# New duration estimates in the list schedule of an attention and two-MLP kernel

## The chip, the cores and the metric

The kernel runs on one core of a Trainium2 chip. Its engines are TensorE (PE, with its weight loads shown apart as PEld), VectorE (DVE), ScalarE (ACT), GpSimd (POOL) and SyncE (SP), which issues the transfers. Each engine executes its own instructions in a fixed order and waits for the others through semaphores. The metric is the time of one execution on the device, in microseconds; several executions are timed and their median is taken.

## The reference

The inputs q, k and v have 2 batches, 8 heads, 768 positions and 64 elements per head. `proj` (64 x 6) hashes every row of q and k into one of 64 buckets, and attention is allowed only inside a bucket. Two linear blocks follow on 1536 tokens of 512 elements.

```python
q_bits = (np.einsum('bhsd,dk->bhsk', q, proj) > 0)      # k_bits alike
mask = q_bucket[:, :, :, None] == k_bucket[:, :, None, :]
scores = np.where(mask, scale * np.matmul(q, k.transpose(0, 1, 3, 2)), -1e9)
attn = softmax(scores)                                  # row maximum taken off first
x = np.matmul(attn, v)                                  # to (1536, 512)
x = ((x @ w1) * (x @ w2)) @ w3 @ w_out                  # d_ff 1024
x = (sigmoid(x @ w_gate) * (x @ w_val)) @ w_out2        # d_ff 1536
```

The weights of the two blocks arrive as 64-bit floats.

## The kernel before, in words

**Attention.** There are 16 heads and six query tiles of 128 per head, so 96 score tiles. Each head's q and k are split into a high and a low part that TensorE can multiply in one pass (`prep`, L389 to L417), the hash bits are computed with three small matmuls per half (`gps`, L387) and are appended to the operands by copies from SBUF to SBUF (L405 to L415). For each score tile TensorE makes four matmuls into one of only two PSUM tiles `s` (L462, L465); VectorE takes the row maximum and prepares the scalars `sm` (L472, L473); ScalarE makes the exponential `e` (L483); TensorE transposes it in pieces of 128 x 128 (`tp`, L516); ScalarE and VectorE copy it out as high and low part `pt` (L519, L521); TensorE multiplies with v (`av`, L534). The two first heads skip the low part.

**Filler.** Between the attention's steps lies work on the weights. Every piece of 128 x 512 weights is loaded by SP into a staging tile `st` (L320) and decoded from 64 bits: ScalarE takes the absolute value and the low bits (L336, L337), GpSimd keeps the sign (L338) and limits the value (`min`, L339), VectorE shifts it (L340) and combines the two (L345, which the profile names a custom instruction). `gen_fill` decodes `w3` and `w_out` and multiplies them into one matrix, `wacc` (L589): ScalarE copies the high part of `w_out` to `wo` (a helper, L278) and GpSimd computes its low part (L584). `gen_first` then decodes `w1` and `w2` and begins with the first 512 tokens of the first linear block (`p` and `y`, L694). 40 of the 76 decodes belong to these two.

**The rest.** `moe` works through the other tokens and the second block, nearly all matmuls of 512 columns (`pa`, `pb` and `m`, L694). It is emitted after the list schedule has been made and isn't part of it.

**What sets the order.** `order_engines` (L47 to L228) takes all instructions emitted so far, that is attention, filler and the beginning of the first block, and simulates their execution. Whenever an engine is free in that simulation, it takes the ready instruction with the lowest priority number: attention's steps and the filler carry numbers that grow from step to step. An instruction is ready when those it depends on have ended, plus a delay by pair of engines (`step`, L93), and when its tile's buffer is free. How long each instruction takes comes from `cost(k)` (L76), and for a transfer from L218 to L221: it begins after a delay or when the transfer before it is done, moves so many bytes per ns, and is known 900 ns later. The order in which each engine took its instructions is then tied down with dependencies (L226 to L228). The durations therefore decide nothing but the order: on the chip each engine keeps it and waits where the next instruction isn't ready. `rings` names for every tile its pool; `psT` and `psS` are the two pools in PSUM, all others lie in SBUF.

Of the kernel before, what the change touches and what calls it, by code (L numbers as in the profile page):

```python
# [29 lines left out]
class Tiles:  # L30
# [3 lines left out]
    rings = {}  # L34
# [12 lines left out]
def order_engines(tc):  # L47
# [8 lines left out]
    rings = Tiles.rings  # L56
    N = len(ins)

    def count(x):
        n = 1  # L60
        for _, c in list(x.ap)[1:]:
            n *= c
        return n

    def region(x):

        b = getattr(x, "bass_ap", None)
        if b is None or b.tensor.name not in rings:
            return None
        ap = [list(p) for p in b.ap]  # L70
        es = mybir.dt.size(b.dtype)
        p0, f0 = divmod(b.offset, ap[0][0]) if ap[0][0] else (0, b.offset)
        f1 = f0 + sum((c - 1) * abs(st) for st, c in ap[1:]) + 1
        return b.tensor.name, p0, p0 + ap[0][1], f0 * es, f1 * es

    def cost(k):  # L76
        i, e, op = ins[k], eng[k], type(ins[k]).__name__
        rd = [x for x in i.ins if hasattr(x, "ap")]
        n = max([count(i.outs[0])] + [count(x) for x in rd[:1]])
        if e == "PE":  # L80
            passes = 1 if "float32r" in str(rd[0].dtype) else 2 if n == 128 else 4
            return n / 2.4 * passes + 2.5
        if e == "Activation":
            return 971 if n == 768 else 50 + n * 0.836
        if e == "Pool":
            return 60 + n * 2.3
        if e == "DVE":
            if op in ("InstTensorTensor", "InstTensorReduce") or (op == "InstTensorScalarPtr" and len(rd) > 1 and count(rd[1]) > 8):
                return 69 + n * 1.04
            return 585 if op == "InstTensorScalarPtr" and n == 384 else 69 + n * 0.52  # L90
        return 600

    step = {("Activation", "DVE"): 145, ("Activation", "PE"): 200, ("Activation", "Pool"): 170, ("DVE", "Activation"): 132,  # L93
# [53 lines left out]
    def blocked(k):  # L147
        for t in opens.get(k, ()):
            g = rings[t][0]
            if slots[g] <= 0 or queue[g][taken[g]] != t:  # L150
                return g
            if g[0] == "mw" and pools.get("wtmp"):
                return "wtmp"
        return None
# [4 lines left out]
    dma = 0.0  # L159

    def wake(g):
        for k in waiting.pop(g, ()):
            heapq.heappush(ready[eng[k]], (ins[k].bass_priority, k))

    def post(t, what, x):
        heapq.heappush(events, (t, next(tick), what, x))
# [4 lines left out]
    while events:  # L171
        now = events[0][0]
        while events and events[0][0] <= now:
            _, _, what, x = heapq.heappop(events)
            if what == "ready":
                heapq.heappush(ready[eng[x]], (ins[x].bass_priority, x))
            elif what == "slot":
                g = rings[x][0]
                slots[g] += 1
                pools[g[0]] -= 1  # L180
                wake(g)
                if not pools[g[0]]:
                    wake(g[0])
            elif what == "end":
                for u in ends[x]:
                    left[u] -= 1
                    at[u] = max(at[u], now + step.get((eng[x], eng[u]), 60))
                    if not left[u]:
                        post(at[u], "ready", u)
                for t in held.get(x, ()):  # L190
                    todo[t] -= 1
                    if not todo[t]:
                        post(now + 200, "slot", t)
        again = True
        while again:
            again = False
            for e in ranks:
                while free[e] <= now and ready[e]:
                    _, k = heapq.heappop(ready[e])
                    g = blocked(k)  # L200
                    if g is not None:
                        waiting.setdefault(g, []).append(k)
                        continue
                    for t in opens.get(k, ()):
                        g = rings[t][0]
                        slots[g] -= 1
                        taken[g] += 1
                        if slots[g] > 0 and waiting.get(g):
                            wake(g)
                            again = True  # L210
                    order[e].append(k)
                    for u in begins[k]:
                        left[u] -= 1
                        at[u] = max(at[u], now)
                        if not left[u]:
                            post(at[u], "ready", u)
                    free[e] = done = now + cost(k)
                    if e == "SP":  # L218
                        n = count(ins[k].outs[0]) * list(ins[k].outs[0].ap)[0][1] * mybir.dt.size(ins[k].outs[0].dtype)
                        dma = max(now + 1080, dma) + n / 360  # L220
                        done = dma + 900  # L221
                    post(done, "end", k)
                    post(free[e], "free", k)
# [8 lines left out]
def lsh_attention_moe_moe2_kernel(  # L232
# [654 lines left out]
    for _ in first:  # L887
        pass
    order_engines(tc)
    prio(0, 200000)  # L890
    att_ctx.close()
# [44 lines left out]
```

## Time and profile before

| what | us or share |
|---|---|
| median of 3 runs (lowest to highest) | 823.49 (823.34 to 823.85) |
| the profiled execution's own time | 825.39 |
| span of its instructions | 823.6 |
| TensorE busy (its weight loads) | 789.6 (660.2) |
| VectorE busy | 467.7 |
| ScalarE busy | 505.9 |
| GpSimd busy | 428.2 |
| mean granted TensorE clock | 0.985 |

The busy times are shares of the whole span. A row of a stage table gives the same numbers for one stretch, so that idle time is the stretch's length less the busy time. Attention and filler lie before about 366 us, the rest after it. In a timeline each line gives start, duration, engine, source line, the tile written and the tile read; the bracket at its end tells how long the engine sat idle just before and which instruction ended the idle time.

### The profile page before, as it was taken

To read this page: it belongs to the slowest core of one execution; us is meant where nothing else is said; L and a number is where in the kernel's file an instruction comes from. 1 tells how busy PE (TensorE), PEld (TensorE's weight loads), DVE (VectorE), ACT (ScalarE), POOL (GpSimd) and SP (SyncE) were. 2 spreads that over 40 slices of the span, in tenths; PEclk is the share of its full clock that TensorE was granted. 3 is DMA by queue.
4 is the path that set the end of the run, shared out by engine and by line. 5 is a ranking of instruction groups with operands and counts; after the bars stand their busy time and mean duration, and the time that the engine had idled before them with its cause. 6 is when DMAs were issued, how large, how long until landed. Compare 5 with 4: busy or idle time off the path is not lost.

```text
span 823.6 us, 11474 instructions
## 1 busy us (share of the span) xinstructions
PE 789.6 (96%) x3984; PEld 660.2 (80%) x3984; DVE 467.7 (57%) x794; ACT 505.9 (61%) x912; POOL 428.2 (52%) x454
## 2 busy tenths in 40 slices
PE   4799899999899999999999999999999999999998
PEld 3577788888799889878888888888888888888886
DVE  6537788887889988985454444654522222222222
ACT  5578888787788887885465656775534333343332
POOL 4567666665556555478355546677532323232320
PEclk9899899999999999999999999999999999999999
DMA  7745557544455644131022213334001000010001
GB/s 247 204 116 164 169 154 197 139 132 114 122 151 155 162 103 129 62 112 52 1 76 77 77 52 101 109 138 138 2 1 51 1 1 0 1 52 0 1 1 51
DMA packets 28585, 74.45 MB, mean 90 GB/s; under 512 B 6128, under 2 KB 8432, under 8 KB 28528
## 3 DMA queue, kind: packets, MB, share of 16 engines
q1 hardware_dynamic: 28528, 73.73, 30.1%
q8 instruction: 31, 0.51, 0.3%
q14 instruction: 26, 0.21, 0.1%
HBM read 52.83 MB, written 3.19 MB: 68 GB/s over the span
## 4 chain that ended last, share of the span: by engine, by line
PE 86%; ACT 5%; DVE 5%; issue 2%; POOL 1%; DMA 1%; SPq 1%; ACTq 0%; POOLq 0%; DVEq 0%
PE m L694 18%; PE pa L694 17%; PE pb L694 17%; PE av L534 8%; PE tp L516 6%; PE p L694 4%; PE wacc L589 4%; PE s L462 4%; PE s L465 3%; PE y L694 3%; ACT e L483 2%; DVE s L472 2%; PE gps L387 2%; DVE pt L521 1%; DMA st<-in_moe_w_dram 1%
## 5 line engine op out<-in xcount | busy, mean ns | idle before, releaser
L734 DVE TENSOR_TENSOR pb<-pb,a 128x512 f32<-128x512 f32 x52 | 36.3, 699 | 179.5 <-PE pb L694 176.2
L472 DVE TENSOR_REDUCE s<-s 128x1 f32<-128x768 f32 x96 | 91.8, 959 | 28.2 <-PE s L465 15.4
L483 ACT ACTIVATE e<-s,sm 128x768 f32<-128x768 f32 x96 | 95.3, 994 | 17.0 <-DVE sm L473 16.3
L516 PE MATMUL tp<-idf,e 128*128 128x128 f32 x576 | 103.2, 279 | 0.0
L688 POOL TENSOR_TENSOR wal<-xall,wah 128x512 fp32r<-128x512 f32 x36 | 46.9, 1304 | 106.2 <-ACT wah L278 106.2
L694 PE MATMUL pa<-x,wah 128*128 128x512 f32 x320 | 99.2, 390 | 0.0
L694 PE MATMUL pb<-x,wbh 128*128 128x512 f32 x320 | 98.6, 389 | 0.0
L338 POOL TENSOR_SCALAR dr<-st 128x512 bf16<-128x512 f32 x76 | 72.3, 961 | 43.4 <-issue 22.6
L519 ACT ACTIVATE pt<-tp 128x512 fp32r<-128x512 f32 (+1 forms) x144 | 82.1, 596 | 20.4 <-PE tp L516 19.1
L534 PE MATMUL av<-pt,spv 128*128 128x256 f32 (+1 forms) x576 | 88.1, 303 | 1.0 <-DVE pt L521 0.9
L521 DVE TENSOR_TENSOR pt<-tp,pt 128x512 fp32r<-128x512 f32 x126 | 83.2, 682 | 9.9 <-ACT pt L519 9.5
L534 PEld LDWEIGHTS av<-pt,spv 128*128 128x128 f32 (+1 forms) x576 | 74.5, 187 | 11.8 <-DVE pt L521 4.0
L516 PEld LDWEIGHTS tp<-idf,e 128*128 128x128 f32 x576 | 73.8, 144 | 9.8 <-issue 1.5
L462 PE MATMUL s<-bk,bq 128*128 128x384 f32 x192 | 64.0, 389 | 14.6 <-ACT e L483 12.8
L589 PE MATMUL wacc<-wo,t 128*128 128x512 f32 x192 | 66.8, 425 | 7.3 <-ACT wo L278 4.7
L694 PEld LDWEIGHTS pa<-x,wah 128*128 128x128 f32 x320 | 60.1, 188 | 13.2
L694 PEld LDWEIGHTS pb<-x,wbh 128*128 128x128 f32 x320 | 60.1, 188 | 12.6
L339 POOL TENSOR_SCALAR da<-da 128x512 f32<-128x512 f32 x76 | 48.1, 637 | 37.8 <-ACT da L336 29.2
L694 PE MATMUL pa<-x,wal 128*128 128x512 f32 x160 | 62.5, 391 | 1.1 <-POOL wal L688 1.1
L694 PE MATMUL pb<-x,wbl 128*128 128x512 f32 x160 | 62.5, 390 | 0.0
L465 PE MATMUL s<-ak,aq 128*128 128x384 f32 x192 | 61.2, 381 | 0.0
L337 ACT ACTIVATE dr<-st 128x512 int16<-128x512 uint32 x76 | 59.7, 786 | 0.1
(137 smaller groups left out, 1794.2 us busy)
## 6 DMA issues: line engine op xcount, KB each, us to landing
st<-in_moe_w_dram SPq DMA_DIRECT2D x32, 512.0 KB, 4.1
st<-in_moe_w_out_dram SPq DMA_DIRECT2D x20, 512.0 KB, 4.2
st<-in_moe_w_gate_dram SPq DMA_DIRECT2D x12, 512.0 KB, 3.3
st<-in_moe_w_val_dram SPq DMA_DIRECT2D x12, 512.0 KB, 3.2
qk<-in_qk_dram SPq DMA_DIRECT2D x15, 384.0 KB, 4.0
rr<-row SPq DMA_DIRECT2D x16, 192.0 KB, 3.5
out_dram<-o SPq DMA_DIRECT2D x12, 256.0 KB, 2.0
ak<-aq SPq DMA_DIRECT2D x15, 192.0 KB, 2.5
```

Source lines behind the costliest of these rows:

```text
L337: act.activation(out=r.bitcast(I16)[:, 0::2], in_=lw, func=AF.Copy, scale=2.0 ** -29)
L338: pool.tensor_scalar(out=r.bitcast(BF16)[:, 1::2], in0=f(hw), scalar1=0.0, scalar2=1.0, op0=ALU.mult, op1=ALU.mult)
L462: pe.matmul(s[:, half, :HS], lhsT=m["bq"][:, qs], rhs=m["bk"][:, ks], start=True, stop=False)
L465: pe.matmul(s[:, half, :HS], lhsT=m["aq"][:, qs], rhs=m["ak"][:, ks], start=False, stop=True)
L472: dve.tensor_reduce(out=one[:, 1:2], in_=s[:, :, :HS], op=ALU.max, axis=AX.XY, negate=True)
L483: act.activation(out=e.rearrange("p (a c) -> p a c", a=2), in_=s[:, :, :HS], func=AF.Exp, bias=sm[:, 1:2], scale=sm[:, 0:1], accum_out=su_ ...
L516: pe.transpose(ps[:, i * P:(i + 1) * P], e_t[g - g % 2 + a][:, c * P:(c + 1) * P], idf)
L519: act.activation(out=dh, in_=src, func=AF.Copy)
L521: dve.tensor_tensor(out=d, in0=src, in1=f(dh), op=ALU.subtract)
L534: pe.matmul(acc[:w.shape[1], :2 * P].rearrange("p (a t) -> p a t", a=2), lhsT=w, rhs=r[:, :, c], start=(c == 0 and i == 0), stop=(c == NT ...
L589: pe.matmul(acc, lhsT=t3[x][:, j], rhs=wo[y][:, j], start=(j == 0 and n == 0), stop=(j == NF1 - 1 and n == 2))
L694: mm = pe.matmul(ps, lhsT=lhs[x], rhs=rhs[y], start=start and n == 0, stop=stop and n == 2)
```

## The change

Two places of `order_engines` get other numbers. `cost` now tells apart whether the operand that is read or the tile that is written lies in PSUM (`banks`), gives GpSimd's subtractions and its other operations formulas of their own, gives VectorE's custom instruction a fixed duration, and shifts TensorE's durations by the kind of matmul. A transfer is taken to begin 1900 ns instead of 1080 after its issue and to move 300 instead of 360 bytes per ns. The instructions, the buffers, the priorities and the delays between engines are as before.

```diff
@@ -77,17 +77,22 @@
         i, e, op = ins[k], eng[k], type(ins[k]).__name__
         rd = [x for x in i.ins if hasattr(x, "ap")]
         n = max([count(i.outs[0])] + [count(x) for x in rd[:1]])
+        banks = [x for x in rd + [i.outs[0]] if (region(x) or ("",))[0] in rings and rings[region(x)[0]][0][0] in ("psT", "psS")]
         if e == "PE":
             passes = 1 if "float32r" in str(rd[0].dtype) else 2 if n == 128 else 4
-            return n / 2.4 * passes + 2.5
+            return n / 2.4 * passes + (16 if passes == 1 else -12 if passes == 2 else 4)
         if e == "Activation":
-            return 971 if n == 768 else 50 + n * 0.836
+            return 971 if n == 768 and banks else 50 + n * (0.836 if banks else 1.0)
         if e == "Pool":
-            return 60 + n * 2.3
+            if op == "InstTensorTensor":
+                return 40 + n * 2.4 if n < 768 else 2200
+            return 100 + n * 1.15
         if e == "DVE":
+            if op == "InstCustomDveAnt":
+                return 720
             if op in ("InstTensorTensor", "InstTensorReduce") or (op == "InstTensorScalarPtr" and len(rd) > 1 and count(rd[1]) > 8):
-                return 69 + n * 1.04
-            return 585 if op == "InstTensorScalarPtr" and n == 384 else 69 + n * 0.52
+                return 69 + n * (1.04 if banks else 1.4)
+            return 585 if op == "InstTensorScalarPtr" and n == 384 else 69 + n * 0.6
         return 600
@@ -217,7 +222,7 @@
                     if e == "SP":
                         n = count(ins[k].outs[0]) * list(ins[k].outs[0].ap)[0][1] * mybir.dt.size(ins[k].outs[0].dtype)
-                        dma = max(now + 1080, dma) + n / 360
+                        dma = max(now + 1900, dma) + n / 300
                         done = dma + 900
```

## Rows read from the trace of the kernel before

**Rows 1.** Stage table: stretch, length, busy us (instructions) per engine, PEclk, DMA share, GB/s.
```profile
0.00:20.00 20.00, 9.19 (x26) 7.62 (x26) 11.87 (x36) 11.40 (x18) 9.20 (x18) 1.00 0.76 248
20.00:48.00 28.00, 22.06 (x103) 16.64 (x104) 14.52 (x26) 18.07 (x35) 16.55 (x21) 0.82 0.69 189
...
76.00:100.00 24.00, 18.73 (x108) 15.99 (x108) 18.76 (x35) 19.37 (x37) 15.79 (x21) 0.86 0.58 170
...
200.00:232.00 32.00, 27.80 (x166) 24.85 (x166) 24.62 (x45) 23.95 (x46) 18.25 (x20) 0.89 0.38 108
232.00:366.00 134.00, 133.60 (x857) 119.67 (x856) 120.18 (x216) 113.06 (x218) 76.75 (x90) 1.00 0.46 127
366.00:823.60 457.60, 452.82 (x1965) 368.28 (x1963) 177.37 (x264) 218.83 (x370) 206.28 (x182) 1.00 0.13 45
```

**Rows 2.** TensorE's waits, whole span: total us, times, longest us.
```profile
PE s L462 <- ACT e L483: 12.8, 9, 3.4
...
PE wacc L589 <- ACT wo L278: 4.7, 2, 2.9
...
PE wacc L589 <- POOL wo L584: 0.9, 1, 0.9
```

**Rows 3.** Timeline of GpSimd, 30 to 47 us: start, duration, instruction.
```profile
31.10 0.61 POOL L339 TENSOR_SCALAR da<-da 128x512 f32<-128x512 f32 x1
...
32.91 0.61 POOL L339 TENSOR_SCALAR da<-da 128x512 f32<-128x512 f32 x1
```

**Rows 4.** Timeline of VectorE in the same stretch.
```profile
32.68 0.67 DVE L409 TENSOR_SCALAR ft<-gps,thr 128x384 fp32r<-128x384 f32 x1
35.38 0.97 DVE L472 TENSOR_REDUCE s<-s 128x1 f32<-128x768 f32 x1 [2.02 <-PE s L465]
...
37.48 0.42 DVE L340 TENSOR_SCALAR da<-da 128x512 uint32<-128x512 uint32 x1
...
38.01 0.69 DVE L345 CUSTOM_DVE_ANT_0 wor<-da,dr 128x1024 uint16<-128x1024 uint16 x1
```

**Rows 5.** Groups of decode steps, 0 to 366 us: busy us, mean ns, idle before.
```profile
L338 POOL TENSOR_SCALAR dr<-st 128x512 bf16<-128x512 f32 x41 | 34.2, 836 | 4.1 <-issue 1.2 <-DVE w3f L345 1.1
...
L339 POOL TENSOR_SCALAR da<-da 128x512 f32<-128x512 f32 x40 | 25.1, 626 | 35.2 <-ACT da L336 28.5 <-DMA qk<-in_qk_dram 4.7
L340 DVE TENSOR_SCALAR da<-da 128x512 uint32<-128x512 uint32 x40 | 22.9, 572 | 7.1 <-POOL da L339 6.9
```

**Rows 6.** Timeline of TensorE, 36 to 47 us.
```profile
39.42 0.79 PE L589 MATMUL wacc<-wo,t 128*128 128x512 f32 x1 [2.91 <-ACT wo L278]
```

**Rows 7.** Timeline of three engines, 84 to 90.6 us.
```profile
84.28 0.61 POOL L339 TENSOR_SCALAR da<-da 128x512 f32<-128x512 f32 x1
...
86.56 0.97 DVE L472 TENSOR_REDUCE s<-s 128x1 f32<-128x768 f32 x1 [1.07 <-PE tp L516]
87.77 0.67 DVE L345 CUSTOM_DVE_ANT_0 wor<-da,dr 128x1024 uint16<-128x1024 uint16 x1
...
89.15 0.54 PE L589 MATMUL wacc<-wo,t 128*128 128x512 f32 x1 [1.81 <-ACT wo L278]
```

**Rows 8.** Transfers by line: issues, KB each, median us from issue to landing.
```profile
st<-in_moe_w_dram SPq DMA_DIRECT2D x32, 512.0 KB, 4.1
...
ak<-aq SPq DMA_DIRECT2D x15, 192.0 KB, 2.5
```

**Rows 9.** Timeline of VectorE and ScalarE, 12 to 16 us.
```profile
13.50 0.22 DVE L473 SCALAR_TENSOR_TENSOR sm<-lim,s 128x2 f32<-128x2 f32 x1
...
14.54 0.97 ACT L483 ACTIVATE e<-s,sm 128x768 f32<-128x768 f32 x1
```

**Rows 10.** Timeline of VectorE and GpSimd, 224 to 227 us.
```profile
224.21 2.24 DVE L632 TENSOR_TENSOR xl<-xall,xh 128x512 fp32r<-128x512 f32 x2
...
225.99 1.10 POOL L338 TENSOR_SCALAR dr<-st 128x512 bf16<-128x512 f32 x1
```

**Rows 11.** Timeline of TensorE, 219 to 226 us.
```profile
221.20 0.44 PE L462 MATMUL s<-bk,bq 128*128 128x384 f32 x1 [2.26 <-ACT e L483]
```

## The prediction

> **What bounds the kernel now.** I read the stage table first. TensorE is the engine that is full: from 20 us on it has work in 78 to nearly 100% of each stretch, and from 232 to 366 us it is idle for only 0.4 us of 134 although VectorE is busy 120.2 us there [rows 1]. From 366 us on, where most of the work lies outside the list schedule, it loses 4.8 us of 457.6 [rows 1]. The set of instructions is the same after the change, so TensorE's work is the same, and the time can move only by TensorE's holes and by the work that runs at the lower clock behind a hole. The holes of the scheduled part are 10.8 us (0 to 20), 5.9 (20 to 48), 5.3 (76 to 100), 4.2 (200 to 232) and 0.4 (232 to 366); the granted clock is 0.82, 0.86 and 0.89 in the middle three, which is at most 0.18 x 28 = 5.0, 0.14 x 24 = 3.4 and 0.11 x 32 = 3.5 us, and 1.00 in the others [rows 1]. That is what a better order can win.
>
> The waits of TensorE say what ends the holes: the score tile waits for the exponential (12.8 us in nine waits), the folded weight product `wacc` waits for ScalarE's copy of a decoded `w_out` (4.7 in two) and for GpSimd's low part (0.9) [rows 2]. The second kind hangs on the decode of weights, and that is the work whose model cost changes most.
>
> **The change, part by part.** It adds no work. It changes the numbers from which each engine's order is drawn up.
>
> GpSimd's two decode steps are the big edit. A step of 512 elements cost 60 + 512 x 2.3 = 1238 ns and now costs 100 + 512 x 1.15 = 689; the pair falls from 2475 to 1378 ns. In the trace GpSimd finished the `min` steps of two decodes at 31.71 and 33.52 us [rows 3]. VectorE was idle for 2.02 us, from 33.35 to 35.38, yet took the shift of the first decode only at 37.48, behind its reductions [rows 4]. The pair is 836 + 626 = 1462 ns in the trace [rows 5]. The old price is 1.0 us above that for the first decode and 2.0 for both, so the old model has them done near 32.7 and 35.5 and had reason to put the reductions first; by the new one they end at 31.6 and 33.4, and shift and combine (0.42 and 0.69 us [rows 4]) fit into the hole. The decoded `w_out` then exists near 34.5 instead of 38.7 (38.01 + 0.69), and ScalarE's copy can follow at once. TensorE's wait of 2.91 us for that copy [rows 6] goes. What is late next there is GpSimd's low part, which TensorE can pass by with transposes. The lower clock costs at most 5.0 us in this stretch [rows 1], and this wait is half of its holes. I take a third, 1.6 us, since the other holes come first and would lower the clock without it. Sum of the first hole: 4.5 us, bounds 0 (it is taken by something else) and 2.9 + 5.0 = 7.9.
>
> The hole at 88 us has the same form: GpSimd was done with a `min` step at 84.89, VectorE stood idle 1.07 us before a reduction at 86.56 and combined the `w_out` only at 87.77; TensorE waited 1.81 us for what follows [rows 7] and 0.9 for GpSimd's part of it [rows 2]. By the old price that step ends 0.6 us later, by the new one within 0.1 us of the measured place. The combine moved into the idle 1.07 us brings the copy forward by up to 1.8 us. I take 2.0 us for wait and clock together, between 0 and 2.7 + 3.4 = 6.1, nearer the low end since the next hole, the scores waiting for the exponential behind it, stays.
>
> Transfers: a 512 KB weight was expected 1080 + 1456 + 900 = 3.44 us after issue and is now 1900 + 1748 + 900 = 4.55, with the transfers one behind another at 300 instead of 360 bytes per ns; the measured median is 4.1. An SBUF copy of 192 KB goes from 2.53 to 3.46, measured 2.5 [rows 8]. So weights are now nearer the truth and the copies farther. At the start ScalarE took two decode steps ahead of the first exponential, whose scalars were ready at 13.72; it began at 14.54 [rows 9]. A model that expects the weights later may turn these round: 0 to 0.8 us, taken 0.4. The copies feed the next head: expected 0.93 us too late, their consumers are put later in TensorE's order. With other work ahead of them that costs nothing; uncovered it is 15 heads x 0.93 = 14 us. I take 0, since in 134 us TensorE idles 0.4 [rows 1]. SP issues in an order drawn from the same model, but no instruction of SP is added, and a load moved on SP is moved with its decode.
>
> ScalarE's copies from SBUF rise by 84 ns (478 to 562), VectorE's combine from 601 to 720 if counted at the 1024 elements that the trace shows (from 335 at 512), its shift from 335 to 376. TensorE: 1464 one-pass matmuls up by 13.5 ns = 19.8 us, 576 transposes down by 14.5 = 8.4, so the modelled TensorE gets 11.4 us longer, which gives the other engines more room in the model. None of these is a cost by itself. They reshuffle everything after the first hole, and the reshuffling has a price: VectorE now meets GpSimd with no reserve. Measured, the two GpSimd steps take 1462 ns against 1378, and VectorE waited for them only 6.9 us in 40 decodes [rows 5]. The reserve that goes is 40 x (1462 - 1378) = 3.4 us of VectorE, and one new hole with its half clock is worth some 2.5 more (the 200 to 232 stretch has 3.5 of clock for two holes). Bounds 0 and 5.9 us, taken 2.9, the middle, as no row shows how much of VectorE's lateness reaches TensorE.
>
> Here a rule bears on the change. While VectorE made two subtractions in 2.24 us, a GpSimd step beside them took 1.10 us [rows 10], where its mean is 0.84 [rows 5]. The Trainium skill's page "SBUF — State Buffer" (Who interferes with whom) says that a VectorE instruction with two SBUF inputs and a GpSimd instruction that reads SBUF shut each other out, whichever comes first running to its end. By that rule no fixed duration fits these two engines, and the trace agrees with it in the rows just named; the time it would give is that of the second rival below.
>
> The holes near 219 us stay: they come when the first phase of the filler ends and four copies of the next phase's input go ahead of an exponential, for which TensorE waits 2.26 us [rows 11]. Their prices rise alike, their priority doesn't change. Term 0, between -2 and +2.
>
> Sum: -4.5 - 2.0 - 0.4 + 2.9 = -4.0 us. The profiled execution took 825.39 us, 1.8 outside its span of 823.6; that gives 821.4 in its terms. The median of the runs is 823.49, 1.9 below the profiled one, so I predict 819.5.
>
> **The rivals.** First, the reshuffling gives back what the two holes give, or the priorities and not the durations set the order there: 823.5. For it: the stretch from 232 us, the longest, has nothing to win. Against: two of the holes have a visible cause in a wrong price.
>
> Second, slower. VectorE's decode steps are placed where GpSimd is expected, GpSimd is late because the two block each other, and VectorE, in order, keeps reduction, scalars and exponential waiting behind the decode, in the stretch from 232 us, where it is busy 120.2 of 134 us. Price: the whole 5.9 us, with the first two holes unchanged: 823.5 + 5.9 = 829.4. It decides from the point where VectorE's waits for GpSimd's `min` step pass about 14 us, twice today's. For it: the longer step beside two subtractions. Against: GpSimd has idle time before most of these steps, and can run ahead.
>
> Third, larger: with transfers and decode right, the holes of 20 to 48 and 76 to 100 us close whole with their clock, about two thirds of 5.9 + 5.0 + 5.3 + 3.4 = 19.6 (hole and half clock overlap), so 13 us: 810.5. Against: scores still wait for exponentials, which have only two score tiles.
>
> **How the numbers follow.** Forecast 0.39 (815 to 822 by itself), no net change 0.17, slower 0.31, larger gain 0.13. A difference within 0.2%, 1.65 us, can't be told from none, so faster means below 821.8 and slower above 825.1. Faster: 0.39 + 0.13 = 0.52, with 0.01 of the no-change case for its edge: 0.53. Same 0.16, slower 0.31. The range goes from 809 (the larger gain) to 829.5 (the slower rival); it leaves out a full 14 us on the copies and a gain beyond 15.
>
> **What would show it.** Right: TensorE's waits for ScalarE's `w_out` copies fall from 4.7 us to under 2; the shift follows GpSimd's `min` within about 1 us near 33 us; the clock in 20 to 48 us above 0.9. Wrong: VectorE's wait for `min` above 14 us, new holes between 232 and 366 us, where 0.4 us stand now, or a clock below 1.00 there. The prediction fails if the holes only change place.

## The result and the profile after

The changed kernel takes 815.98 us (median of four executions, 812.86 to 816.30) against 823.67 for the kernel before, a ratio of 0.990 with a 95% interval of 0.987 to 0.992. The forecast was the right way and 4.0 us; the kernel gained 7.7. The profiled execution happens to be the quickest of the four, 812.86 us with a span of 811.1, and that of before is slower than its median, so the two traces differ by 12.5 us and what is read from them overstates the gain.

The stage table of the kernel after, with the columns of [rows 1], and under it TensorE's largest waits as in [rows 2]:

```profile
0.00:20.00 20.00, 9.98 (x27) 7.31 (x28) 13.26 (x38) 12.26 (x19) 9.87 (x18) 0.87 0.76 266
20.00:48.00 28.00, 26.01 (x138) 20.20 (x137) 17.66 (x29) 23.16 (x45) 23.89 (x30) 0.91 0.82 214
...
76.00:100.00 24.00, 23.43 (x148) 20.05 (x146) 22.81 (x44) 21.25 (x42) 17.74 (x24) 1.00 0.82 230
...
200.00:232.00 32.00, 28.27 (x185) 25.07 (x184) 29.53 (x51) 27.06 (x53) 17.26 (x22) 1.00 0.60 161
232.00:366.00 134.00, 132.09 (x810) 115.04 (x809) 117.40 (x201) 111.66 (x215) 81.33 (x87) 1.00 0.45 120
```

```profile
PE s L467 <- ACT e L488: 9.7, 8, 2.5
...
PE wacc L594 <- ACT wo L283: 2.0, 1, 2.0
```

The hole of 20 to 48 us fell from 5.9 to 2.0 us and that of 76 to 100 from 5.3 to 0.6, where the clock is whole again [rows 1]. In return 232 to 366 us has 1.9 us of hole where it had 0.4. TensorE executes 138 and 148 matmuls in the two early stretches instead of 103 and 108: work came forward. What brought it is seen at 28 us, in a timeline of four engines of the kernel after (compare [rows 3, 4, 6]):

```profile
28.12 0.61 POOL L344 TENSOR_SCALAR da<-da 128x512 f32<-128x512 f32 x1
...
28.77 0.43 DVE L345 TENSOR_SCALAR da<-da 128x512 uint32<-128x512 uint32 x1 [2.66 <-POOL da L344]
...
29.34 0.76 POOL L343 TENSOR_SCALAR dr<-st 128x512 bf16<-128x512 f32 x1
...
29.40 1.18 DVE L350 CUSTOM_DVE_ANT_0 wor<-da,dr 128x1024 uint16<-128x1024 uint16 x1
...
30.18 0.88 POOL L344 TENSOR_SCALAR da<-da 128x512 f32<-128x512 f32 x1
...
30.62 0.63 ACT L283 ACTIVATE wo<-wor 128x512 fp32r<-128x512 f32 x1 [1.02 <-DVE wor L350]
...
31.30 0.50 PE L594 MATMUL wacc<-wo,t 128*128 128x512 f32 x1 [1.99 <-ACT wo L283]
```

VectorE takes the shift 0.04 us after GpSimd's `min` ends (28.73), not 5.8 us after it as before. The first `wacc` runs at 31.3 us instead of 39.4. The eight decodes of `w_out` show how far this goes. The two fences are the combine step of these decodes, before and after, with the shortest, median and longest duration in ns and the first and last start in us:

```profile
L345 DVE CUSTOM_DVE_ANT_0 wor<-da,dr x8: 672/693/1448, 38.0 to 87.8; 128x1024 uint16<-128x1024 uint16 x8
```

```profile
L350 DVE CUSTOM_DVE_ANT_0 wor<-da,dr x8: 686/920/1807, 29.4 to 65.3; 128x1024 uint16<-128x1024 uint16 x8
```

All eight are done 22.5 us earlier. The attention ends earlier too: VectorE's last low part `pt` starts at 344.8 us instead of 356.7:

```profile
L521 DVE TENSOR_TENSOR pt<-tp,pt x126: 640/681/693, 68.3 to 356.7; 128x512 fp32r<-128x512 f32 x126
```

```profile
L526 DVE TENSOR_TENSOR pt<-tp,pt x126: 669/681/695, 63.4 to 344.8; 128x512 fp32r<-128x512 f32 x126
```

That is 11.9 of the 12.5 us between the two profiled executions. Behind it the two differ by 0.6 us.

### The profile page after: what moved, and what is told of

Its sections match the earlier page's. It is cut to its first block, busy times and chain, and to the rows that moved or that the text cites. A ratio compares the mean times of both kernels' runs of the same rounds, so it can differ in the third digit from the quotient of the medians.

```text
span 811.1 us, 11465 instructions
## 1 busy us (share of the span) xinstructions
PE 785.6 (97%) x3984; PEld 653.5 (81%) x3984; DVE 470.0 (58%) x794; ACT 505.5 (62%) x912; POOL 431.4 (53%) x454
## 4 chain that ended last, share of the span: by engine, by line
PE 80%; DVE 8%; ACT 4%; POOL 4%; DMA 2%; issue 2%; SPq 1%; ACTq 0%; DVEq 0%; POOLq 0%
PE m L699 18%; PE pa L699 18%; PE pb L699 18%; PE av L539 6%; PE tp L521 5%; PE p L699 4%; PE wacc L594 3%; PE s L467 3%; PE s L470 2%; DVE s L477 2%; PE y L699 2%; DVE pt L526 2%; ACT e L488 1%; PE gps L392 1%; DMA st<-in_moe_w_dram 1%
## 5 line engine op out<-in xcount | busy, mean ns | idle before, releaser
L521 PE MATMUL tp<-idf,e 128*128 128x128 f32 x576 | 107.0, 275 | 1.7 <-DVE xall L552 1.0
L539 PE MATMUL av<-pt,spv 128*128 128x256 f32 (+1 forms) x576 | 85.2, 297 | 1.8 <-DVE pt L526 1.8
L521 PEld LDWEIGHTS tp<-idf,e 128*128 128x128 f32 x576 | 72.9, 141 | 12.5 <-DVE xall L552 2.0
L539 PEld LDWEIGHTS av<-pt,spv 128*128 128x128 f32 (+1 forms) x576 | 72.3, 182 | 11.9 <-DVE pt L526 4.5
L344 POOL TENSOR_SCALAR da<-da 128x512 f32<-128x512 f32 x76 | 50.3, 666 | 45.5 <-ACT da L341 38.7
L699 PEld LDWEIGHTS pa<-x,wah 128*128 128x128 f32 x320 | 60.1, 188 | 13.2
L699 PEld LDWEIGHTS pb<-x,wbh 128*128 128x128 f32 x320 | 60.1, 188 | 12.6
L470 PE MATMUL s<-ak,aq 128*128 128x384 f32 x192 | 63.2, 385 | 0.0
```

The lines of the kernel that those rows point to most:

```text
L470: pe.matmul(s[:, half, :HS], lhsT=m["aq"][:, qs], rhs=m["ak"][:, ks], start=False, stop=True)
L521: pe.transpose(ps[:, i * P:(i + 1) * P], e_t[g - g % 2 + a][:, c * P:(c + 1) * P], idf)
L539: pe.matmul(acc[:w.shape[1], :2 * P].rearrange("p (a t) -> p a t", a=2), lhsT=w, rhs=r[:, :, c], start=(c == 0 and i == 0), stop=(c == NT ...
L699: mm = pe.matmul(ps, lhsT=lhs[x], rhs=rhs[y], start=start and n == 0, stop=stop and n == 2)
```

## The experiments

Theory 1: the price of GpSimd's decode steps held the filler back, and it alone makes the gain. Rivals: the later landing of transfers does; any new set of prices reshuffles the order and what comes out is luck; the decodes of the second filler phase carry a part. Every kernel was timed in rounds beside the kernel before on the same chip; times are medians, ratios carry their 95% interval.

**GpSimd's prices and the landing, one at a time.**

```diff
 only_pool = before, with
-            return 60 + n * 2.3
+            if op == "InstTensorTensor":
+                return 40 + n * 2.4 if n < 768 else 2200
+            return 100 + n * 1.15
 no_pool = after, with these lines put back
 only_dma = before, with
-                        dma = max(now + 1080, dma) + n / 360
+                        dma = max(now + 1900, dma) + n / 300
 no_dma = after, with this line put back
```

> The kernel before with GpSimd's new prices alone. Theory 1 (the holes at 28 to 40 and 88 us stood because GpSimd's decode steps were priced at 1238 ns and take 836 and 626): most of the gain of 7.7 us, so 817 to 819; TensorE's waits for ScalarE's copies of w_out under 2.5 us against 4.7. Rival (any new set of prices throws the order and the sum is what falls out): anywhere between 817 and 828, with the w_out waits not tied to the time. Second rival (the landing times did it): 823 to 825, holes of before 48 us unchanged.

Measured 815.94 us, 0.990 (0.988 to 0.992): the whole gain and more than theory 1 said. TensorE no longer waits for the `w_out` copies among its large waits.

> The kernel after with GpSimd's prices put back to 60 + 2.3 n for all its instructions. Theory 1: back to 821 to 824, and the w_out waits back above 4 us. Second rival (landing times): stays at 816 to 817. Reshuffling rival: anywhere.

822.23 us, 0.997 (0.995 to 0.998), as theory 1 said; but the marker failed, TensorE's wait for the copies is 1.3 us and not above 4. The filler is late all the same: the last `w_out` combine is at 84.0 us.

> The kernel before with the later landing of transfers alone. Theory 1: 822 to 825, as no GpSimd price changes; at most 0.8 us from the first exponential. Second rival: 816 to 818.

820.50 us, 0.995 (0.994 to 0.997): more than theory 1 allowed and far less than the rival said.

> The kernel after with the landing of transfers put back to 1080 ns and 360 bytes per ns. Theory 1: 815 to 818. Second rival: 822 to 824 with the holes of 20 to 48 us back.

821.54 us, 0.996 (0.994 to 0.997): theory 1 missed by 3.5 us. The rival's mark, the holes of 20 to 48 us, didn't come back either (1.9 us). The trace has a new hole of 4.3 us in 48 to 76 us, with a granted clock of 0.88. In the timeline of this kernel GpSimd sits 3.07 us before scaling the next head's q and k, whose load SP issued at 50.81 and which landed 7.3 us later, and VectorE waits 4.49 us for the decode step behind it; the stage table of the same kernel stands under it:

```profile
50.81 0.59 SPq L370 DMA_DIRECT2D qk<-in_qk_dram  x1
...
58.28 0.99 POOL L405 TENSOR_SCALAR qk<-qk 64x384 f32<-64x384 f32 x2 [3.07 <-DMA qk<-in_qk_dram]
...
61.26 1.48 DVE L345 TENSOR_SCALAR da<-da 128x512 uint32<-128x512 uint32 x1 [4.49 <-POOL da L344]
```

```profile
48.00:76.00 28.00, 23.71 (x118) 16.84 (x117) 16.58 (x28) 20.19 (x39) 17.97 (x22) 0.88 0.58 161
```

Whether that is what an early landing costs or an accident was asked by two more kernels: GpSimd's prices and the landing together, and no_dma with 5 ns more on ScalarE's prices.

> The kernel before with GpSimd's new prices and the later landing, all else old. If the later landing is worth something of itself beside GpSimd's prices: 810 to 814. If not: 815 to 818, as with GpSimd's prices alone.

816.55 us, 0.991 (0.989 to 0.993): the landing adds nothing to GpSimd's prices.

> The kernel after with the old landing (821.5 us), shaken by 5 ns on ScalarE's prices but the exponential's. If the early landing itself costs: 820 to 824, and GpSimd waiting above 2 us for q and k before 100 us. If it was an accident of that order: 816 to 819.

819.66 us, 0.995 (0.994 to 0.997), between the two forecasts; GpSimd waits 2.3 us for the q and k of later heads before 100 us, the longest 1.3, and 2.9 us of hole are left in 48 to 76 us. The kernel after with the same shake and the new landing takes as long (after_act5 below, 819.35). So the landing by itself gave 3.4 us (only_dma), 5.6 (no_dma), 0.3 here and -0.6 (pool_dma against only_pool): nothing that stands clear of the accidents of an order.

**Which of GpSimd's prices.**

```diff
 decode_cheap = before, with
+            if "TensorScalar" in op and n == 512:
+                return 689
             return 60 + n * 2.3
 others_cheap = before, with
+            if not ("TensorScalar" in op and n == 512):
+                return (40 + n * 2.4 if n < 768 else 2200) if op == "InstTensorTensor" else 100 + n * 1.15
             return 60 + n * 2.3
 first24, last16 = decode_cheap, with nth[k] numbering GpSimd's decode steps, two per decode
+            if k in nth and nth[k] < 48:      # last16: nth[k] >= 48
+                return 689
```

> The kernel before with only GpSimd's two decode steps of 512 elements at 689 ns, its other instructions at the old price. Theory 1 (the overpriced decode steps held the filler back, from 20 to 100 us): 815 to 818, VectorE and GpSimd busier by 3 us or more in 20 to 48 and in 76 to 100 us, TensorE's hole of 76 to 100 us under 2. Rival (it is the steps that prepare q and k, 384 elements, 943 to 542 ns): 821 to 824.

815.37 us, 0.989 (0.988 to 0.991): one number changed for two instructions makes the whole gain. Against [rows 1] VectorE is busier by 3.0 and 4.7 us in the two early stretches, and the hole of 76 to 100 us is 0.75 us, as theory 1 said; GpSimd is busier by 4.5 and only 1.9, so one of its marks failed.

```profile
20.00:48.00 28.00, 25.20 (x131) 19.15 (x130) 17.55 (x28) 22.60 (x44) 21.05 (x26) 0.94 0.69 204
...
76.00:100.00 24.00, 23.25 (x153) 20.08 (x152) 23.41 (x44) 20.71 (x40) 17.69 (x24) 1.00 0.71 203
```

> The kernel before with GpSimd's new prices for everything but the two decode steps. Theory 1: 821 to 825, hole of 76 to 100 us above 3.5 us. Rival (preparation of q and k): 815 to 818.

820.93 us, 0.996 (0.995 to 0.998). The time lies at the lower edge of theory 1; the hole of 76 to 100 us is 3.0 us and not above 3.5. This kernel too has its last `w_out` combine at 68.7 us, as early as where the gain is whole, and yet gains only 3.1 us: an early `w_out` isn't enough. Most of its hole is a wait for ScalarE's copy `t` of a decoded `w3`:

```profile
85.49 0.51 PE L591 MATMUL wacc<-wo,t 128*128 128x512 f32 x1 [2.43 <-ACT t L280]
```

> The kernel before with the price of 689 ns on GpSimd's decode steps of the first 24 decodes alone (w3 and w_out). Theory 1 (the early filler was held back, the gain is made before 100 us): 814 to 818, as with all decodes cheap. Rival (the later decodes carry half of it): 818.5 to 821.

815.64 us, 0.990 (0.988 to 0.991).

> The kernel before with the price of 689 ns on GpSimd's decode steps of the last 16 decodes of the schedule alone (w1 and w2). Theory 1: 821 to 824, what a meaningless shake gives. Rival: 817 to 820.

825.48 us, 1.002 (1.001 to 1.003): 1.6 us slower than before, above both forecasts and no gain. The gain is all made with the first 24 decodes. The stage rows of 20 to 100 us show the difference, first24 and then last16, with VectorE busy 64.2 and 48.9 us and GpSimd 63.8 and 51.3:

```profile
20.00:100.00 80.00, 74.31 (x429) 59.14 (x428) 64.22 (x107) 66.70 (x127) 63.83 (x79) 0.98 0.69 197
```

```profile
20.00:100.00 80.00, 67.59 (x371) 52.91 (x370) 48.86 (x89) 60.44 (x114) 51.34 (x64) 0.94 0.59 167
```

**The other prices.**

```diff
 no_pe = after, with TensorE's old line
-            return n / 2.4 * passes + (16 if passes == 1 else -12 if passes == 2 else 4)
+            return n / 2.4 * passes + 2.5
 tp_old = after, with 2.5 for two passes;  one_old = after, with 2.5 for one pass
 no_av = after, with ScalarE's and VectorE's old lines
```

> The kernel after with TensorE's old prices. Theory 1: 814 to 818, within 2 us of after, since TensorE is the engine that is full and the others follow it. Rival (all prices matter alike, each undone one loses): 819 to 823.

811.49 us, 0.985 (0.983 to 0.986), better than either forecast: TensorE's new prices cost 4.5 us.

> The kernel after with the transposes' old price (109 instead of 95 ns, and the trace has four transposes in 0.44 us). If the too low price of the transposes is what costs: 811 to 814. If it is the one-pass matmuls' price: 815 to 819.

818.01 us, 0.993 (0.991 to 0.994).

> The kernel after with the one-pass matmuls' old price (n / 2.4 + 2.5 instead of + 16). If the one-pass price is what costs: 811 to 814. If the transposes' price does: 815 to 819.

812.02 us, 0.986 (0.984 to 0.987): it is the price of the one-pass matmuls that costs. no_pe and one_old beat both kernels clearly.

> The kernel after with the old prices of ScalarE and VectorE. Theory 1: 814 to 818. Rival (all prices matter alike): 819 to 823, with VectorE's custom step too cheap again and exponentials late behind it.

818.90 us, 0.994 (0.992 to 0.995): the loss of 2.9 us is 0.9 more than theory 1 allowed, but within what a shake does. There is a second pair with no other difference than these prices: pool_dma (816.55) has the old ones, no_pe (811.49) the new, 5.1 us apart. So the new prices of ScalarE and VectorE seem to gain 3 to 5 us, about what TensorE's take back, and the gain of after is not GpSimd's alone.

**What a shake is worth.** Prices moved by a few ns without meaning give another order and measure the luck in it: 2 ns on GpSimd in before, 5 ns on ScalarE (all but the exponential) in before, in after and in no_pe.

```diff
 before_pool2:  return 62 + n * 2.3
 *_act5:        55 + n * 0.836    # after and no_pe: 55 + n * (0.836 if banks else 1.0)
```

> The kernel before with 2 ns on every GpSimd price, a change that means nothing: it measures what a mere reshuffling is worth. Theory 1 (a named price matters): within 2 us of 823.7, hole of 76 to 100 us stays above 3.5 us. Rival (the order of before is an unlucky one and any other gains): 818 to 821.

822.15 us, 0.997 (0.996 to 0.999).

> The kernel before with 5 ns on every ScalarE price but the exponential's, again without meaning. Theory 1: within 2 us of 823.7. Rival (unlucky order): 818 to 821.

822.13 us, 0.997 (0.996 to 0.998). Two shakes of before gain 1.7 and 1.8 us, so its order is slightly unlucky, by no more than that; in the first the hole of 76 to 100 us is 4.6 us.

> The kernel after with 5 ns on every ScalarE price but the exponential's. Theory 1 (prices matter): 814 to 818. Rival (a lucky order that any shake loses): 819 to 822. This gives the spread that the differences of a few us between the part kernels must be held against.

819.35 us, 0.994 (0.992 to 0.996): 3.4 us lost, as the rival said and more than theory 1 allowed. So differences of 3 us between these kernels mean nothing by themselves, and the order of after is somewhat lucky.

> The kernel after with TensorE's old prices (811.5 us in its run), shaken by 5 ns on every ScalarE price but the exponential's. If TensorE's new prices are worse in themselves: 809 to 814. If the 811.5 was a lucky order: 815 to 818.

812.81 us, 0.986 (0.985 to 0.988). The orders with the old one-pass price lie at 811.5, 812.0 and 812.8, those with the new one, everything else as in after or with the transposes' price changed, at 816.0, 818.0 and 819.4. The two groups don't meet.

The rival that any new set of prices is luck can be held against all twenty kernels. The thirteen in which at least the first 24 decodes are cheap lie from 811.5 to 821.5 us, the seven others from 820.5 to 825.5. Only no_dma, the slowest of the thirteen, is above the quickest of the seven.

**Where all of them gain.** For a profiled execution each, its own time, the last `w_out` combine, the first subtraction of the second filler phase (`xl`), VectorE's last low part `pt`, and TensorE's holes from 20 to 100 us:

| kernel | own time | last `w_out` | first `xl` | last `pt` | holes |
|---|---|---|---|---|---|
| before | 825.4 | 87.8 | 216.7 | 356.7 | 11.2 |
| last16 | 825.0 | 86.8 | 216.0 | 356.8 | 12.4 |
| only_dma | 820.5 | 84.1 | 213.4 | 352.2 | 7.8 |
| no_dma | 820.3 | 66.6 | 209.9 | 352.3 | 6.9 |
| no_av | 820.1 | 67.5 | 207.5 | 352.0 | 2.6 |
| others_cheap | 819.8 | 68.7 | 209.6 | 351.1 | 8.9 |
| only_pool | 818.1 | 66.6 | 205.3 | 349.7 | 4.1 |
| tp_old | 816.7 | 60.1 | 207.3 | 350.0 | 3.2 |
| first24 | 815.4 | 68.2 | 206.9 | 346.8 | 5.7 |
| after | 812.9 | 65.3 | 204.2 | 344.8 | 2.6 |
| one_old | 811.9 | 66.4 | 207.6 | 343.9 | 4.7 |
| no_pe | 811.1 | 66.1 | 202.4 | 342.2 | 2.8 |

Own time less the last `pt` is 466.7 us in tp_old and 467.8 to 468.9 in the nineteen others. What the order does is done when attention ends. Neither the last `w_out` nor the early holes put the kernels in order by themselves: no_av and tp_old have both early and few, and lose afterwards.

## Why the forecast was half of the gain

The bound was read rightly: TensorE's work is the same, 785.6 us busy against 789.6, and the time went with its holes (8.5 of the 12.5 us between the traces) and the clock. The main cause was read rightly as well: the price of GpSimd's two decode steps is by itself enough for the gain (decode_cheap), and the first instance at 28 us went as said, with the shift next to `min`.

**The step that failed is the size of the second hole.** The prediction took 2.0 us for it, near the low end, since "the next hole, the scores waiting for the exponential behind it, stays". It didn't stay. In the trace of after the stretch of 76 to 100 us lost 4.7 of its 5.3 us of hole, and its granted clock rose from 0.86 to 1.00, worth at most the 3.4 us. The likely reason is that the holes were treated one by one, each with a combine pulled into the gap beside it. The decodes come one after another: each that the schedule lets end earlier brings the next forward, and after eight of them the `w_out` part is 22.5 us ahead, so that at 88 us nothing waits for a decode any more. first24 shows that the decodes of `w3` and `w_out` give the whole gain, and last16 that without them nothing is won; that it is their accumulated lead which does it, rather than one of them, is read from the starts in the traces and was not tried apart, and others_cheap shows that an early `w_out` alone is not enough.

The medians share the miss out more evenly than the traces. The two holes were given 6.5 us, and decode_cheap, which changes that price alone, gained 8.7. The other terms were given 2.5 us against the change, and after gained 1.0 less than decode_cheap. So 2.2 us of the 3.7 that were missed lie in the holes and 1.5 in the terms against them, both less than a shake can move.

**The first hole** was sized 4.5 us, 2.9 of waiting and 1.6 of clock. Measured in the traces: 3.9 us of hole and at most 2.5 of clock (0.82 to 0.91 of 28 us), so it was sized too low as well. The forecast wait of under 2 us for the `w_out` copies came out at 2.0. The clock forecast, above 0.9, came out at 0.91.

**The term against it**, 2.9 us for VectorE meeting GpSimd without reserve, had the wrong mechanism. VectorE's wait for GpSimd's `min` step fell. The decode steps of 0 to 366 us in the kernel after (compare [rows 5]):

```profile
L343 POOL TENSOR_SCALAR dr<-st 128x512 bf16<-128x512 f32 x42 | 34.4, 823 | 2.4
...
L344 POOL TENSOR_SCALAR da<-da 128x512 f32<-128x512 f32 x42 | 29.2, 696 | 43.0 <-ACT da L341 37.9 <-DMA aq<-ft 3.4
L345 DVE TENSOR_SCALAR da<-da 128x512 uint32<-128x512 uint32 x40 | 25.4, 636 | 3.7 <-POOL da L344 3.7
```

The wait fell from 6.9 to 3.7 us, far from the 14 from which the second rival was to decide. The two steps did take a little longer together, 1519 ns against 1462, and the median combine of `w_out` rose from 693 to 920 ns. The Trainium skill's page "SBUF — State Buffer" (Who interferes with whom) says that a VectorE instruction with two SBUF inputs contends with a GpSimd instruction that reads SBUF. The first combine, with two such inputs, took 1.18 us while two decode steps of GpSimd ran beside it, from 29.34 and 30.18 us, which agrees; that this is what made the combines longer wasn't tried apart. But GpSimd reaches the `min` step early, since it idles 43.0 us before these steps. After 100 us 2.5 us of hole were added, 1.0 in 100 to 200 and 1.5 in 232 to 366, which was one of the prediction's signs of being wrong; TensorE's largest wait there is for exponentials (5.6 us from 100 to 366 us, 4.4 before).

**TensorE's prices** were said to cost nothing by themselves. They cost 4.5 us (no_pe against after) or 6.5 (both shaken), and it is the one-pass price of + 16 ns. The waits for exponentials between 100 and 366 us are 5.6 us in after and 1.8 in one_old, in the next two fences, but 4.5 in no_pe, so that these waits are the path of the loss isn't shown:

```profile
PE s L467 <- ACT e L488: 5.6, 5, 2.4
PE av L539 <- DVE pt L526: 1.8, 4, 0.8
```

```profile
PE s L467 <- ACT e L488: 1.8, 4, 0.9
PE av L539 <- DVE pt L526: 1.3, 4, 0.5
```

What stays open is why a price nearer to the trace gives the worse order (two of these 512-column matmuls one behind the other stand 0.23 us apart in the timelines, and the new price is 229 ns, the old one 216).

**The start and the landing** were given 0.4 us. The landing alone gains 3.4 us over before, 1.7 of which a shake gives too, and nothing beside GpSimd's prices. **The holes near 219 us** stay, as said: they lie at 204 to 212 us now and are 3.1 us. But the lower clock behind them is gone (200 to 232 us: 0.89 to 1.00, at most 3.5 us), for which the prediction had put 0, and the first 20 us fell from 1.00 to 0.87, at most 2.6 us.

So the sum read -4.5 - 2.0 - 0.4 + 2.9. In the two traces the holes are -3.9 - 4.7 in the two early stretches, -0.8 at the start, +2.0 from 100 to 366 us and -1.1 behind it, 8.5 us in all; TensorE's busy time for the same matmuls fell by another 4.0, with the mean granted clock at 0.993 instead of 0.985. The single bounds of the clock above add up to more than these 4.0, as they count idle time too. The quickest execution of after lies 3.1 us below its median, and what makes executions of one order differ by that much was not found.

## What to carry to other kernels

In a list schedule a price that is far off can cost more than the gap beside its step, on the least loaded engine too: here it also held open a hole 50 us later. So don't size its gain hole by hole. Shake a schedule's prices by a few ns before believing a difference of 3 us between two orders. Nearer prices are not better orders by themselves: undo each kind alone, as one of them, TensorE's, cost 4 us here.

## What the runs showed that was not expected

**Two holes of one length, one with the lower clock behind it.** Two stretches of equal kind, the stage rows of before and then of after, in each the 4 us with the largest hole near the filler's second phase and the 4 us behind it:

```profile
220.00:224.00 4.00, 1.74 (x10) 1.34 (x10) 3.91 (x8) 3.99 (x8) 2.24 (x4) 0.82 0.61 180
224.00:228.00 4.00, 3.66 (x15) 3.50 (x16) 4.00 (x8) 3.10 (x7) 2.93 (x3) 0.50 0.00 0
```

```profile
208.00:212.00 4.00, 1.58 (x11) 1.29 (x10) 4.00 (x9) 4.00 (x9) 1.47 (x2) 1.00 0.56 175
212.00:216.00 4.00, 4.00 (x32) 3.86 (x32) 4.00 (x8) 3.95 (x8) 3.83 (x5) 1.00 0.20 55
```

TensorE's hole was 2.3 us in the one (it ended at 221.20 us) and 2.4 in the other (211.19). In before the granted clock went to 0.50, the lower level of 1.2 GHz; in after it stayed at 2.4. The twelve `av` matmuls behind the hole, before and then after, took 2.91 and 1.66 us:

```profile
226.28 2.91 PE L534 MATMUL av<-pt,spv 128*128 128x256 f32 x12
```

```profile
212.26 1.66 PE L539 MATMUL av<-pt,spv 128*128 128x256 f32 x12
```

Before has a second hole, of 1.40 us up to 224.34, but the clock had fallen ahead of it: it is 1.00 up to 222.5 us and 0.50 from 223.0 to 229.0. So the length of the hole doesn't tell the two apart; what does isn't shown. A forecast that prices a hole must leave the clock as a chance.

**Transfers landed later where the filler gained.** Between 20 and 100 us the median landing of a 512 KB piece of `w3` rose from 3.9 to 6.6 us, and that of the copy that ends a head's preparation from 4.4 to 7.7, in rows of the transfers of before and then of after:

```profile
st<-in_moe_w_dram SPq DMA_DIRECT2D x7, 512.0 KB, 3.9
...
bq<-aq SPq DMA_DIRECT2D x4, 192.0 KB, 4.4
```

```profile
st<-in_moe_w_dram SPq DMA_DIRECT2D x10, 512.0 KB, 6.6
...
bq<-aq SPq DMA_DIRECT2D x5, 192.0 KB, 7.7
```

The engines of the transfers were busy 59% of that stretch before and 77% after. So a landing time fitted to one order need not hold for the next.
